# GpSimd waits by semaphore for the vector instruction planned before it at their shared port

## The chip, the cores and the metric

The kernel runs on one core of a Trainium2 chip. The metric is device time in microseconds of that core, the median of three runs. A core has a tensor engine (TensorE, PE in the profile), a vector engine (VectorE, DVE), a scalar engine (ScalarE, ACT), a general engine (GpSimd, POOL) and a queue engine for transfers (SyncE, SP). Each takes its own instructions strictly in order, and they wait for each other by semaphores. The planner in this kernel treats VectorE and GpSimd as sharing a port to on-chip memory.

## The reference

Attention by random features over 8 batches, 8 heads, 576 positions and 64 dimensions with 128 features, and behind it a bilinear feed-forward part over the 4608 tokens of width 512:

```python
def phi(x):                                     # q and k, scaled by 64 ** -0.25
    h = einsum('bhsd,md->bhsm', x, omega) - sum(x * x, -1) / 2
    return exp(h - max(h, -1)) / sqrt(m)
kv  = einsum('bhsm,bhsd->bhmd', phi(k), v)
num = einsum('bhsm,bhmd->bhsd', phi(q), kv)
den = einsum('bhsm,bhm->bhs', phi(q), sum(phi(k), 2)) + 1e-6
x = (num / den) as 4608 x 512
out = ((x @ w1) * (x @ w2)) @ w3 @ w_out        # 512 -> 1024 -> 1024 -> 512
```

## The kernel before

The 4608 tokens are 36 chunks of 128. For precision most matrix operands are split into two 16-bit halves, a high part and the rest, and each product is made of three: high by high, high by low, low by high. So nearly every tensor passes a step that writes the high part (mostly ScalarE) and one that writes the rest (VectorE or GpSimd).

For each chunk the kernel loads q, k and v; splits them (hl, vhl); projects q and k on TensorE into PSUM (pa); takes the maximum (s_nm on VectorE), subtracts it (e on VectorE or within ScalarE's exponential), and splits the result into eq and ek. GpSimd writes most of the low parts of eq and ek by a tensor_tensor of 128x1024 in `in_parts`. The halves of eq are turned by transfers (eqT) and multiplied with kv; VectorE divides (xs), and the result is scaled, split (xhl) and turned by transfers (xT). From chunk 6 on two chunks go together: `pair_turn` lets GpSimd form four sums of xs (128x256 each), after which ScalarE writes the high parts of two xhl tiles and VectorE the rest. The gate multiplies xT with w1 and w2 in a scheme of seven products a pair (weights in w12b, sums of weights in mag); results pass ScalarE and VectorE as asb; GpSimd makes some of their products and the low part of the hidden tile (big). The last product with the joined weights Wb gives the output, which ScalarE scales (o). GpSimd also writes constants into vhl by small memsets.

Nothing runs as written: class `Plan` records every operation with its tiles, then `order` tries several list schedules with estimated costs and returns all operations in the order of their planned starts. `Plan.locks` names those that it takes to need the shared port: everything that GpSimd computes, and VectorE's instructions with wide operands in on-chip memory only (not those that read or write PSUM, no reductions). `forward` never lets two of these overlap in the plan. `fill` adds dummy matmuls in long planned gaps of the first 200 us. `emit` calls `Op.fire` for each operation: the instruction is tied behind its predecessor on its own engine, and `held` lists other operations whose end it waits for by semaphore. Before the change `held` serves a few first loads alone. On the chip nothing else keeps the two engines to the planned turns at the port: each starts when its own data are there.

All instructions are issued from one helper line, L172, so the profile's rows are told apart by tile and shape.

Of the kernel before, what the change touches and what calls it, by code (L numbers as in the profile page):

```python
# [249 lines left out]
class Plan:  # L250
# [77 lines left out]
    def cost(self, op):  # L328
# [20 lines left out]
        if op.lane == "vector":  # L349
# [7 lines left out]
            else:  # L357
                t = 68 + 0.53 * m + 45 * len(thin)
            return t * MARGIN, t * MARGIN + 85
        if op.lane == "scalar":  # L360
            t = (51 if any(a.space == PSUM for a in op.ins) else 93) + 0.834 * m + 92 * len(thin)
            t += 70 if "accum_out" in op.kwargs else 0
            return t * MARGIN, t * MARGIN + 95
        if op.method == "memset":
# [3 lines left out]
        else:  # L368
            t = 100 + 1.0 * m
        return t * MARGIN, t * MARGIN + 50  # L370

# [115 lines left out]
    def order(self):  # L487

        ops = self.ops
        costs = {o: self.cost(o) for o in ops}  # L490
        for o in ops:
            o.locks = self.locks(o)

        def turned(deps):
            after = {o: [] for o in ops}
            for o in ops:
                for d in deps[o]:
                    after[d].append(o)
            return after

        rank = {o: o.index for o in ops}
        best = None
        self.seen = []
        plain = {o: set(o.deps) for o in ops}
        later = turned(plain)
        scale = TURN0
        dice = random.Random(SEED)
        for n in range(ROUNDS + TRIES):
            if n >= ROUNDS:
                rank = {o: r + dice.gauss(0.0, SPREAD) for o, r in best[3].items()}  # L510
            tried = rank
            start, total, slot = self.forward(rank, plain, later, costs, True, scale=scale)
            self.seen.append(total)
            deps = self.chained(start, slot)
            after = turned(deps)
            for m in range(INNER + 1):
                if m:
                    start, total, _ = self.forward(rank, deps, after, costs, scale=1.0)
                    self.seen.append(total)
                if best is None or total < best[0]:  # L520
                    best = total, start, slot, tried
                back = {o: -start[o] - costs[o][0] for o in ops}
                late, _, _ = self.forward(
                    back,
                    {o: set(after[o]) for o in ops},
                    {o: list(deps[o]) for o in ops},
                    costs,
                    backwards=True,
                )
                rank = {o: -late[o] - costs[o][0] for o in ops}  # L530
                scale = 1.0
        _, start, slot, _ = best
        for g, k in slot.items():
            g.slot = k
        start = dict(start)
        self.fill(start, costs)
        return sorted(start, key=lambda o: (start[o], o.index))

    def fill(self, start, costs):


        busy = {}
        for g in self.gens:
            if g.ops and g.tag == "pm":
                a = min(start[o] for o in g.ops)
                b = max(start[o] + costs[o][0] for o in g.ops) + 2 * HOP + 170
                busy.setdefault(g.slot, []).append((a, b))
        line = sorted((o for o in self.ops if o.lane == "tensor"), key=lambda o: start[o])
        end = FIRST
        for o in line:  # L550
            a, b = end, start[o]
            end = b + costs[o][0]
            n = int((b - a - GAP) // 216)
            if n <= 0 or a > UNTIL:
                continue
            idle = [
                (max([y for x, y in t if y <= a + HOP] + [0]), k)
                for k, t in busy.items()
                if not any(x < b and y > a for x, y in t)
            ]  # L560
            if not idle:
                continue
            gen = Gen(self.bank_pool, "pm", [128, 512], F32, 4)
            gen.slot = min(idle)[1]
            out = View(gen, gen.pool.base(gen, gen.slot))
            stuff = Op("tensor", "matmul", (), {})
            stuff.parts = [
                Op("tensor", "matmul", (out, self.ones, self.ones[:, 0:1].broadcast_to([128, 512])),
                   {"start": True, "stop": True})
                for _ in range(n)  # L570
            ]
            stuff.index = o.index
            start[stuff] = a + 1
# [17 lines left out]
SPLIT = True  # L591
HOP = 80
MARGIN = 1.04
ROUNDS = 2
TRIES = 14
SPREAD = 500.0
# [1036 lines left out]
```

## Time and profile before

| what | value |
|---|---|
| device time, median of 3 runs | 767.67 us (766.59 to 767.84) |
| the profiled execution | 767.67 us |
| its span in the trace | 765.9 us |
| PE busy | 742.4 us (97%) |
| DVE busy | 561.1 us (73%) |
| ACT busy | 529.4 us (69%) |
| POOL busy | 317.0 us (41%) |

A busy time counts an instruction from its start to its end, so it holds the time in which an engine stands inside an instruction. Idle time is put down to the instruction or transfer whose end released the engine. The shares are means over very different stages: VectorE is nearly full from 100 to 360 us and has little to do in the last 150, where TensorE works alone. The windows view gives the busy times stage by stage, the waits view who was waited for, and the timeline single instructions; names are the program's tiles, written tile first, then what is read.

### The profile page before, as it was taken

The page shows a single profiled execution, that of the slowest core. Times are in us where ns is not written, and L with a number is a line of the kernel's source. Part 1 is how long each engine was busy: PE and PEld are TensorE (multiplying, and loading weights), DVE is VectorE, ACT ScalarE, POOL GpSimd, SP SyncE. Part 2 cuts the span into 40 slices and gives each one's busy share as a digit, 9 for nine tenths or more (in the row PEclk, how much of TensorE's full clock was granted, in tenths as well). Part 3 has the DMA queues.
Part 4 walks back from the last instruction along what each step waited for, and adds up shares of the span by engine and source line. Part 5 has one row for each costly group of instructions (what it writes and reads, how often), then busy time and mean ns, then how long its engine had stood idle before and what let it go on. Part 6 is the DMA issues. An engine that isn't in the chain of part 4 may idle for free.

```text
span 765.9 us, 24815 instructions
## 1 busy us (share of the span) xinstructions
PE 742.4 (97%) x10639; PEld 579.4 (76%) x10639; DVE 561.1 (73%) x1078; ACT 529.4 (69%) x1069; POOL 317.0 (41%) x306
## 2 busy tenths in 40 slices
PE   8999999999999899988999999999999999999998
PEld 4455678968777879776978877887768887878885
DVE  4568999998999998998898799869773644422220
ACT  6999969878777988877887979966764444322221
POOL 1100102216455475655767645754553434412321
PEclk9999999999999999999999999999999999999999
DMA  9889984426432785545656556661545233312101
GB/s 337 298 311 304 247 183 86 75 67 153 105 58 71 159 170 131 118 98 126 139 144 128 118 115 153 131 122 40 114 78 95 62 87 64 63 43 50 43 15 42
DMA packets 165678, 94.60 MB, mean 124 GB/s; under 512 B 139776, under 2 KB 140160, under 8 KB 165568
## 3 DMA queue, kind: packets, MB, share of 16 engines
q1 hardware_dynamic: 165056, 91.97, 51.2%
q8 instruction: 83, 1.36, 0.8%
q10 hardware_dynamic: 432, 0.79, 0.3%
q14 instruction: 27, 0.22, 0.1%
q0 software_dynamic: 80, 0.26, 0.1%
HBM read 49.35 MB, written 9.44 MB: 77 GB/s over the span
## 4 chain that ended last, share of the span: by engine, by line
PE 63%; DVE 22%; DMA 6%; ACT 6%; issue 3%; SPq 0%; DVEq 0%; ACTq 0%
PE pm L172 53%; PE pa L172 10%; DMA xT<-xhl 4%; DVE s_nm L172 3%; DVE xhl L172 3%; DVE asb L172 2%; DVE big L172 2%; DVE hl L172 2%; ACT e L172 2%; DVE vhl L172 2%; DVE e L172 2%; DVE w12b L172 1%; DVE s_mx L172 1%; DVE xs L172 1%; DMA big<-w3T 1%
## 5 line engine op out<-in xcount | busy, mean ns | idle before, releaser
L172 PE MATMUL pm<-xT,w12b 128*128 128x128 f16 (+1 forms) x3840 | 245.4, 223 | 3.8 <-DMA xT<-xhl 2.4
L172 PEld LDWEIGHTS <-w12b 128*128 128x128 f16 x3840 | 227.6, 98 | 13.7 <-issue 2.8
L172 PE MATMUL pm<-Wb,big 128*128 128x512 f16 (+1 forms) x888 | 192.1, 373 | 0.0
L172 PEld LDWEIGHTS <-big 128*128 128x128 f16 x888 | 85.0, 98 | 92.8 <-issue 0.7
L172 PE MATMUL pm<-xT,mag 128*128 128x128 f16 x2160 | 136.1, 220 | 2.9 <-ACT asb L172 2.8
L172 PEld LDWEIGHTS <-mag 128*128 128x128 f16 x2160 | 124.6, 98 | 6.6 <-issue 3.5
L172 POOL TENSOR_TENSOR big<-asb,big 128x512 f16<-128x512 f32 x72 | 91.7, 1283 | 90.2 <-ACT big L172 71.1
L172 POOL TENSOR_TENSOR eq<-e,eq 128x1024 f16<-128x1024 f32 x31 | 69.5, 2243 | 96.8 <-DVE eq L172 67.7
L172 DVE TENSOR_REDUCE s_nm<-pa 128x8 f32<-128x1024 f32 x72 | 86.7, 1216 | 24.1 <-PE pa L172 23.6
L172 ACT ACTIVATE e<-pa,s_nm,s_es 128x128 f32<-128x128 f32 x240 | 87.9, 465 | 10.6 <-DVE s_nm L172 9.5
L172 POOL TENSOR_TENSOR ek<-e,ek 128x1024 f16<-128x1024 f32 x28 | 63.2, 2256 | 65.0 <-ACT ek L172 49.5
L172 POOL TENSOR_TENSOR asb<-asb,asb 128x512 f32<-128x512 f32 x30 | 40.0, 1332 | 109.4 <-DVE asb L172 100.0
L172 DVE SCALAR_TENSOR_TENSOR asb<-pm,asb 128x512 f32<-128x512 f32 x60 | 41.1, 685 | 50.2 <-PE pm L172 49.7
L172 DVE TENSOR_TENSOR asb<-pm,asb 128x512 f32<-128x512 f32 x72 | 48.8, 681 | 38.9 <-PE pm L172 38.3
L172 ACT CAST big<-asb 128x512 f16<-128x512 f32 x72 | 43.8, 621 | 48.3 <-DVE asb L172 35.0
L172 DVE SCALAR_TENSOR_TENSOR xhl<-xs,s_p2r,xhl 128x768 f16<-128x768 f32 (+2 forms) x36 | 50.3, 1396 | 26.7 <-ACT xhl L172 26.7
L172 PE MATMUL pm<-mag,mag 128*128 128x512 f32 x128 | 58.7, 601 | 0.0
L172 ACT ACTIVATE xhl<-xs,s_p2r 128x768 f16<-128x768 f32 (+2 forms) x36 | 35.8, 993 | 32.3 <-DMA xT<-xhl 25.5
L172 POOL TENSOR_TENSOR xs<-xs 128x256 f32<-128x256 f32 x60 | 48.0, 816 | 21.2 <-DVE xs L172 18.9
L172 ACT ACTIVATE o<-pm,oscs 128x512 f32<-128x512 f32 (+1 forms) x37 | 25.2, 680 | 41.4 <-PE pm L172 39.1
L172 ACT COPY asb<-pm 128x512 f32<-128x512 f32 x60 | 34.9, 592 | 24.0 <-POOL big L172 13.0
L172 PE MATMUL pa<-om,hl 64*128 64x128 f16 x1320 | 45.6, 217 | 4.9 <-DVE xs L172 3.7
(115 smaller groups left out, 1040.2 us busy)
## 6 DMA issues: line engine op xcount, KB each, us to landing
vraw<-v SPq DMA_DIRECT2D x36, 256.0 KB, 3.9
qraw<-qT SPq DMA_DIRECT2D x35, 256.0 KB, 2.8
out<-o SPq DMA_DIRECT2D x34, 256.0 KB, 3.1
big<-w3T SPq DMA_DIRECT2D x8, 1024.0 KB, 7.5
kraw<-kT SPq DMA_DIRECT2D x32, 256.0 KB, 2.9
big<-w SPq DMA_DIRECT2D x8, 1024.0 KB, 7.0
big<-wo SPq DMA_DIRECT2D x3, 1024.0 KB, 5.8
eqT<-eq SPq DMA_TRANSPOSE x72, 3.5
```

The source lines that it names most:

```text
L172: p.real = getattr(lanes[p.lane], p.method)(*args, **{k: real(a) for k, a in p.kwargs.items()})
```

## The change

After the planning a new step, `turns`, walks through all port-using operations in the order of their planned starts. It remembers the last one of VectorE. Each GpSimd operation that follows gets that one into its `held` list, if it doesn't depend on it by its data anyway and if its planned start lies less than `NEAR` = 2500 ns behind the planned end of the vector operation. The tensor order, the tiles, the buffers and every engine's order of instructions stay the same. 179 of GpSimd's operations get such a wait: 56 memsets of vhl, one of mag, 35 low parts of eq and ek, 33 sums of xs and 54 instructions on asb (products and low parts of big). GpSimd's program has 109 semaphore instructions after it, and 72 before; ScalarE's has two fewer.

```diff
--- before.py
+++ after.py
@@ -534,7 +534,17 @@
             g.slot = k
         start = dict(start)
         self.fill(start, costs)
+        self.turns(start, costs)
         return sorted(start, key=lambda o: (start[o], o.index))
+
+    def turns(self, start, costs):
+
+        last = None
+        for o in sorted((o for o in self.ops if o.locks), key=lambda o: (start[o], o.index)):
+            if o.lane == "vector":
+                last = o
+            elif last and last not in o.deps and start[o] - start[last] - costs[last][0] < NEAR:
+                o.held.append(last)
 
     def fill(self, start, costs):
 
@@ -591,6 +601,7 @@
 SPLIT = True
 HOP = 80
 MARGIN = 1.04
+NEAR = 2500.0
 ROUNDS = 2
 TRIES = 14
 SPREAD = 500.0
```

Two places on GpSimd's queue, written as instruction, output<-inputs, size, and in brackets the engines whose semaphores the instruction waits for (DMAHW is a transfer; the numbers only name the counters, and the value waited for is not shown). The first is at 200.7 to 215 us of the trace: eq0 and ek are low parts of features, big0 the low parts of hidden tiles. Before:

```order
L172 TENSOR_TENSOR eq0_101<-e1_305,eq0_101 128x1024 [waits DMAHW2_49,Activation_49]
L172 TENSOR_TENSOR big0_77<-asb2_465,big0_77 128x512 [waits Activation_49]
L172 TENSOR_TENSOR ek4_410<-e0_90,ek4_410 128x1024 [waits Activation_49]
L172 TENSOR_TENSOR big0_77<-asb1_419,big0_77 128x512 [waits Activation_49]
L172 TENSOR_TENSOR eq0_101<-e1_305,eq0_101 128x1024 [waits DMAHW0_49,DVE_49]
L172 TENSOR_TENSOR ek5_671<-e0_90,ek5_671 128x1024 [waits Activation_49]
```

and now:

```order
L172 TENSOR_TENSOR eq0_101<-e1_305,eq0_101 128x1024 [waits DMAHW2_49,DVE_49]
L172 TENSOR_TENSOR big0_77<-asb2_465,big0_77 128x512 [waits Activation_49]
L172 TENSOR_TENSOR ek4_410<-e0_90,ek4_410 128x1024 [waits DVE_49,Activation_49]
L172 TENSOR_TENSOR big0_77<-asb1_419,big0_77 128x512 [waits DVE_49,Activation_49]
L172 TENSOR_TENSOR eq0_101<-e1_305,eq0_101 128x1024 [waits DMAHW0_49,Pool_49]
L172 TENSOR_TENSOR ek5_671<-e0_90,ek5_671 128x1024 [waits DVE_49,Activation_49]
```

The order is the same. The first eq0, the ek parts and the second big0 now wait for VectorE as well. Where a wait vanished from a row, as on the second eq0, a row ahead of it waits for a later vector instruction already.

The second is at 330 to 351 us; xs0 are the four sums of a pair. Before:

```order
L172 TENSOR_TENSOR eq0_101<-e1_305,eq0_101 128x1024 [waits DMAHW4_49,DVE_49,Pool_49]
L172 TENSOR_TENSOR ek3_328<-e0_90,ek3_328 128x1024 [waits Activation_49]
L172 TENSOR_TENSOR big0_77<-asb1_419,big0_77 128x512
L172 TENSOR_TENSOR xs0_105<-xs0_105 128x256 [waits DVE_49]
L172 TENSOR_TENSOR big0_77<-asb2_465,big0_77 128x512 [waits Activation_49,Pool_49]
L172 TENSOR_TENSOR xs0_105<-xs0_105 128x256 [waits Pool_49]
L172 TENSOR_TENSOR xs0_105<-xs0_105 128x256 [waits DVE_49]
L172 TENSOR_TENSOR xs0_105<-xs0_105 128x256 [waits Pool_49]
L172 TENSOR_TENSOR eq0_101<-e1_305,eq0_101 128x1024 [waits DMAHW5_49,DVE_49]
L172 TENSOR_TENSOR asb0_89<-asb0_89,asb1_419 128x512
```

and now:

```order
L172 TENSOR_TENSOR eq0_101<-e1_305,eq0_101 128x1024 [waits DVE_49,DMAHW4_49,Activation_49,Pool_49]
L172 TENSOR_TENSOR ek3_328<-e0_90,ek3_328 128x1024 [waits Activation_49]
L172 TENSOR_TENSOR big0_77<-asb1_419,big0_77 128x512
L172 TENSOR_TENSOR xs0_105<-xs0_105 128x256 [waits DVE_49]
L172 TENSOR_TENSOR big0_77<-asb2_465,big0_77 128x512 [waits Activation_49,Pool_49]
L172 TENSOR_TENSOR xs0_105<-xs0_105 128x256 [waits Pool_49]
L172 TENSOR_TENSOR xs0_105<-xs0_105 128x256 [waits DVE_49] x2
L172 TENSOR_TENSOR eq0_101<-e1_305,eq0_101 128x1024 [waits DMAHW5_49,DVE_49,Activation_49]
L172 TENSOR_TENSOR asb0_89<-asb0_89,asb1_419 128x512
```

Again nothing moved. The first eq0 and the last waited for VectorE before, for their own high part, and wait for a later vector instruction now; the fourth xs0 waited for GpSimd's third sum only, and now for VectorE (equal rows are shown as one, with x2).

## Rows read from the trace of the kernel before

Times in a timeline are us from the span's start.

**Rows 1.** Stage, length, busy us (count) of PE, PEld, DVE, ACT, POOL; clock, DMA, GB/s.
```profile
195.00:255.00 60.00, 53.72 (x827) 43.72 (x825) 59.76 (x105) 43.19 (x87) 32.83 (x31) 0.98 0.39 86
299.00:355.00 56.00, 51.34 (x846) 41.00 (x842) 54.14 (x100) 45.24 (x90) 33.92 (x33) 1.00 0.55 126
355.00:555.00 200.00, 196.59 (x3319) 162.66 (x3313) 168.57 (x329) 157.95 (x315) 119.01 (x112) 0.99 0.55 117
555.00:671.00 116.00, 114.38 (x1752) 92.80 (x1749) 61.15 (x132) 52.16 (x101) 49.31 (x43) 1.00 0.40 74
```

**Rows 2.** Timeline of VectorE, 329 to 355: start us, duration us, instruction, count.
```profile
330.55 5.17 DVE L172 SCALAR_TENSOR_TENSOR vhl<-vraw,s_s,vhl 128x512 f16<-128x512 f32 x2
...
343.47 0.75 DVE L172 SCALAR_TENSOR_TENSOR vhl<-vraw,s_s,vhl 128x512 f16<-128x512 f32 x1
...
345.46 1.01 DVE L172 SCALAR_TENSOR_TENSOR xhl<-xs,s_p2r,xhl 128x768 f16<-128x768 f32 x1
...
349.01 3.15 DVE L172 SCALAR_TENSOR_TENSOR xhl<-xs,s_p2r,xhl 128x1024 f16<-128x1024 f32 x1
352.09 1.75 DVE L172 SCALAR_TENSOR_TENSOR vhl<-vraw,s_s,vhl 64x512 f16<-64x512 f32 x1
353.76 0.67 DVE L172 TENSOR_TENSOR xs<-pa,s_gr 128x512 f32<-128x512 f32 x1
```

**Rows 3.** Timeline of VectorE, 518 to 521.
```profile
518.92 1.28 DVE L172 SCALAR_TENSOR_TENSOR xhl<-xs,s_p2r,xhl 128x1024 f16<-128x1024 f32 x1 [1.21 <-ACT xhl L172]
```

**Rows 4.** Timeline of GpSimd, 329 to 355 (in brackets: idle before).
```profile
330.10 2.52 POOL L172 TENSOR_TENSOR eq<-e,eq 128x1024 f16<-128x1024 f32 x1 [5.37 <-issue]
...
338.63 2.11 POOL L172 TENSOR_TENSOR xs<-xs 128x256 f32<-128x256 f32 x3
348.51 2.57 POOL L172 TENSOR_TENSOR eq<-e,eq 128x1024 f16<-128x1024 f32 x1 [7.77 <-DVE eq L172]
```

**Rows 5.** Timeline of VectorE: first and last blocked instructions, and one at 544.
```profile
195.47 1.22 DVE L172 CAST eq<-e 128x1024 f16<-128x1024 f32 x1
...
250.24 3.14 DVE L172 SCALAR_TENSOR_TENSOR xhl<-xs,s_p2r,xhl 128x1024 f16<-128x1024 f32 x1
...
309.87 0.47 DVE L172 TENSOR_SCALAR s_nm<-s_nm,s_es 128x8 f32<-128x8 f32 x1
...
544.66 2.10 DVE L172 TENSOR_SCALAR s_nm<-s_nm,s_es 128x8 f32<-128x8 f32 x1
```

**Rows 6.** What TensorE waited for in 195 to 255: us, times, longest.
```profile
PE pm L172 <- ACT asb L172: 0.6, 1, 0.6
PE pm L172 <- ACT junk L172: 0.6, 1, 0.6
```

**Rows 7.** What TensorE waited for, 299 to 355.
```profile
PE pm L172 <- ACT asb L172: 0.4, 1, 0.4
```

**Rows 8.** What TensorE waited for, 355 to 555.
```profile
PE pm L172 <- ACT asb L172: 1.5, 2, 1.3
PE pa L172 <- DVE xs L172: 0.8, 2, 0.5
```

**Rows 9.** The same view as rows 1, in two stretches behind idle spells of TensorE.
```profile
253.00:257.00 4.00, 3.72 (x40) 3.72 (x41) 3.90 (x8) 2.44 (x5) 1.16 (x1) 0.57 0.81 182
355.00:359.00 4.00, 4.00 (x51) 3.90 (x45) 3.02 (x4) 2.85 (x6) 1.67 (x2) 0.57 0.25 46
```

**Rows 10.** Timeline of TensorE, 355 to 361.
```profile
355.27 2.58 PE L172 MATMUL pm<-xT,mag 128*128 128x128 f16 x24
...
359.58 1.50 PE L172 MATMUL pm<-xT,mag 128*128 128x128 f16 x24
```

**Rows 11.** Timeline of ScalarE, 329 to 355.
```profile
347.57 1.17 ACT L172 ACTIVATE xhl<-xs,s_p2r 128x1024 f16<-128x1024 f32 x1
```

**Rows 12.** Timeline of GpSimd, 517 to 521.5.
```profile
519.12 0.92 POOL L172 MEMSET vhl<- 64x8 f16 x10
```

**Rows 13.** Groups by line and form, VectorE: count, busy us, mean ns, idle before.
```profile
L172 DVE TENSOR_REDUCE s_nm<-pa 128x8 f32<-128x1024 f32 x72 | 86.7, 1216 | 24.1 <-PE pa L172 23.6
```


## The prediction, made before the changed kernel ran

> **What bounds the kernel now.** Read first the busy times by stage, then what TensorE waits for in each stage, and only then single instructions. By stage [rows 1] TensorE is the busiest engine, but it is not always busy: it stands 60.00 - 53.72 = 6.28 us in 195 to 255, 56.00 - 51.34 = 4.66 us in 299 to 355, 200.00 - 196.59 = 3.41 us in 355 to 555 and 116.00 - 114.38 = 1.62 us in 555 to 671. The reader is to see which engine is full in the two stages that lose most: VectorE, with 59.76 of 60 and 54.14 of 56 us, while GpSimd is at 32.83 and 33.92. So there VectorE sets the end of a step and TensorE waits for it; a microsecond of VectorE given back in those stages shortens the run, until TensorE's own idle time is used up. Elsewhere VectorE has slack and TensorE bounds.
>
> Part of VectorE's full time is not work. Two splits of v in 330.55 take 5.17 us, the same form takes 0.75 alone in 343.47; the split of x in 349.01 takes 3.15 [rows 2], the same form 1.28 in 518.92 [rows 3]. Beside the long ones a GpSimd tensor_tensor began about 0.5 us before: eq in 330.10 and in 348.51 [rows 4]. VectorE's instruction ends when GpSimd's has ended plus its own length: 348.51 + 2.57 = 351.08, plus 1.28 gives 352.36, and it ended in 352.16. So whoever holds the port first makes the other wait. In 195 to 255 there are 12 vector instructions over 75 ns longer than their form's usual time, together 10.7 us; in 299 to 355 there are 8, together 9.2 us (the first and the last of each stage: [rows 2, 5]).
>
> **The change, part by part.** It moves nothing and adds no work to VectorE; it holds 179 GpSimd instructions until the port-using vector instruction planned just before them has ended. A block goes where the GpSimd instruction that made it now waits for the blocked instruction or a later one. Going through the blocked ones with the plan's order, that is so for 10 of the 12 in 195 to 255 (10.0 of 10.7 us), among them those that the first eq0 and the second big0 of the first place shown with the change had blocked, and for 6 of the 8 in 299 to 355 (8.2 of 9.2 us).
>
> One place step by step. The eq in 330.10 now waits for the second of the two v splits. These then take 0.75 each, so VectorE is through in 332.05 and not in 335.72: 3.7 us earlier. GpSimd's eq starts in about 332.1, 2.0 us later, but runs without a block. The eq in 348.51 waits for the half-tile v split of 352.09: VectorE needs 1.28 and about 0.75 us from 349.01 and is through in about 351.0 instead of 353.8, so the xs of 353.76, on which TensorE's longest wait of this stage ends, comes 2.8 us earlier than it did. What is late next is then TensorE itself, with its matmuls before that wait.
>
> By stage, what VectorE gets back (10.0 and 8.2 us) is above what TensorE loses (6.28 and 4.66), so the whole loss could go. I do not count waits that another engine ended and that I can't follow to a blocked vector instruction: in 195 to 255 the two of 0.6 behind ScalarE [rows 6], leaving 6.28 - 1.2 = 5.1; in 299 to 355 the 0.4 behind ScalarE [rows 7], leaving 4.66 - 0.4 = 4.25. In 355 to 555 I count the 0.8 that VectorE's xs ended and 1.3 of the 1.5 behind ScalarE's asb [rows 8], because ScalarE stood there behind the blocked s_nm of 544.66, which took 2.10 us for eight numbers a row [rows 5]: 2.1. In 555 to 671 nothing. Sum 5.1 + 4.25 + 2.1 = 11.45 us.
>
> **The clock.** Right after the two longest idle spells the granted clock falls: 0.57 on the mean in 253 to 257 and in 355 to 359 [rows 9], which is the lower level, 1.2 GHz, for most of each stretch. A group of 24 matmuls takes 2.58 us in 355.27 and 1.50 in 359.58 [rows 10]. At 0.57 four microseconds lose 4 x 0.43 = 1.7, less the little that was idle: 1.6 and 1.7. Both stretches follow spells that the change shortens, so I count both: 3.3 us. Bounds: nothing, if a spell stays long enough to bring the lower level, and 3.3.
>
> **What it costs.** GpSimd starts later. Its added waits have no row before, so from both sides: nothing where the vector instruction has ended anyway, and at most the delay seen by laying the held pairs side by side. The longest is the fourth sum of xs, last of the three in 338.63 [rows 4]. It now waits for the split of x in 345.46, which ends in 346.47 [rows 2]; with 0.70 for the sum it is done in 347.2 and not in 340.74, 6.5 us late. Its reader, ScalarE's xhl, starts in 347.57 [rows 11], so even this one is hidden, by 0.4 us. Behind a held instruction everything on GpSimd's queue stands too, the eq and ek parts and the next sums; GpSimd is idle for 22 of 56 us in this stage, which is the cover [rows 1]. I take nothing for the waits, the value that the longest of them shows, and keep 6 us for the range. TensorE has no wait that GpSimd ended in any of these stages.
>
> Of the 179 waits, 56 hold memsets of vhl. Ten such memsets in 519.12 [rows 12] lie inside the split of x in 518.92, which takes its 1.28 us all the same [rows 3]. The Trainium skill (SBUF — State Buffer, Who interferes with whom) states that a vector instruction with two SBUF inputs contends with a GpSimd instruction that reads SBUF and not with one that only writes it; by that rule these 56 waits buy nothing and only hold GpSimd's queue, and the trace agrees at this place. The sum is the same by rule and by row: no gain was booked for them, and their delay falls under the waits above.
>
> **The sum.** The profiled execution took 767.67 us, which is the median of the three runs too (its span is 765.9, 1.8 lie around it). 767.67 - 11.45 - 3.3 = 752.9 us.
>
> **Rivals.**
> - Half of it. VectorE is freed, but the next thing in line, ScalarE's activations or the transposes of x and eq, ends the step almost as late. For it: ScalarE has 45.24 of 56 us, and part of TensorE's waits in 195 to 255 end on it [rows 1, 6]. Against it: VectorE is given back 1.6 and 1.8 times what TensorE stands (10.0 to 6.28, 8.2 to 4.66). Half of 11.45 and one of the two clock stretches: 767.67 - 5.7 - 1.7 = 760.3 us.
> - The block only moves. GpSimd must read for its 33.9 us within those 56 somewhere, and after the wait it may meet the next port-using vector instruction instead. For it: GpSimd's instructions are up to 2.6 us long and VectorE leaves no gap. Against it: much of VectorE's work does not use the port, such as the reductions from PSUM, at 1216 ns on the mean with 86.7 us in all [rows 13], and the plan lays GpSimd's instructions beside these; holding them brings them back there. It would give 767.7 us, no change.
> - Slower: the sums of xs. They feed ScalarE's xhl, the transpose and TensorE's matmuls, and there is one set of four for each of 15 pairs of chunks. Where the vector instruction waited for is itself late, or ScalarE ready earlier than in 347.57, the 6.5 us of the fourth sum comes through to TensorE save for its 0.4 of cover: 6.1 us a pair. Three such pairs cost 18.3 and outweigh 14.75 of gain: 771.2 us. It decides from the third pair on. For it: cover of 0.4 us is thin. Against it: with VectorE earlier the instruction waited for is earlier too.
>
> **How the numbers follow.** Forecast 0.62, half 0.22, the block moves 0.08, slower 0.08. About 0.2%, 1.5 us, is what a measurement of this kernel can tell from no change. So faster 0.62 + 0.22 = 0.84, same 0.08, slower 0.08. Low end: all of TensorE's idle time in the four stages (15.97) and both clock stretches, 767.67 - 19.3 = 748.4. High end: past half, with the 6 us kept for the waits, 760.3 + 6 = 766.3, up to the edge of no change. That leaves out the last two cases, 0.16, and little below.
>
> **What would show it.** Right: in the changed profile the v splits near 330 take 0.75 each and the x split near 349 takes 1.28; VectorE's busy time falls by some 30 us, GpSimd's idle time ended by VectorE grows; TensorE's idle time in 195 to 355 falls below 4 us; the granted clock has no fall near 253 and 355. Wrong: VectorE's blocked instructions are as many as before, only others (the block moves); ScalarE's xhl waits on GpSimd's xs by several us a pair (slower); or VectorE's time falls and TensorE's waits stay, ended by ScalarE or transposes (half).

## The result, and the profile after

The changed kernel takes 753.59 us (752.89 to 754.26, median of 4), the kernel before 767.15 beside it: ratio 0.9823, 95% interval 0.9806 to 0.984. Forecast were 752.9 us, in a range of 748.4 to 766.3. The profiled execution took 754.26 us with a span of 752.5, so 13.4 us less span than before.

The page's busy times of the changed kernel, engine by engine:

```profile
PE 738.1 (98%) x10639; PEld 576.2 (77%) x10639; DVE 534.7 (71%) x1078; ACT 528.7 (70%) x1069; POOL 296.1 (39%) x306
```

TensorE's idle time went from 765.9 - 742.4 = 23.5 to 752.5 - 738.1 = 14.4 us: 9.1 of the 13.4. The other 4.3 are TensorE's busy time, with as many matmuls; the two falls of the clock [rows 9] are not in this execution. VectorE is busy for 534.7 us and not 561.1, GpSimd for 296.1 and not 317.0, with the same instructions: both stood inside their instructions before.

By stage, in the columns of [rows 1] (the windows are the same times; TensorE's work of before now comes earlier, by 0.2 us at 195, 6 at 253, 10 at 355 and 15 at 555):

```profile
195.00:255.00 60.00, 58.09 (x959) 48.62 (x958) 57.54 (x112) 49.47 (x100) 30.50 (x33) 1.00 0.51 102
255.00:299.00 44.00, 43.06 (x799) 36.28 (x797) 37.77 (x71) 37.61 (x77) 23.09 (x27) 1.00 0.70 147
299.00:355.00 56.00, 54.38 (x806) 41.82 (x802) 48.37 (x106) 48.01 (x99) 30.74 (x24) 1.00 0.68 133
355.00:555.00 200.00, 199.35 (x3389) 163.72 (x3386) 164.38 (x346) 156.42 (x309) 114.78 (x116) 1.00 0.59 118
555.00:671.00 116.00, 113.18 (x1739) 93.52 (x1737) 51.49 (x104) 48.90 (x96) 46.36 (x40) 1.00 0.34 67
```

TensorE stands 1.91, 0.94, 1.62, 0.65 and 2.82 us in them, where it stood 6.28, 0, 4.66, 3.41 and 1.62. VectorE is no longer full in 299 to 355: 48.37 us against 54.14. The granted clock is 1.00 in all five. What TensorE still waits for in 195 to 255, then in 299 to 355, then in 555 to 671 (us, times, longest):

```profile
PE pm L172 <- DMA xT<-xhl: 1.6, 1, 1.6
PE pa L172 <- DMA eqT<-eq: 0.3, 1, 0.3
```

```profile
PE pm L172 <- ACT asb L172: 1.6, 1, 1.6
```

```profile
PE pm L172 <- DVE asb L172: 1.5, 1, 1.5
PE pa L172 <- ACT e L172: 0.6, 2, 0.4
PE pm L172 <- ACT asb L172: 0.5, 1, 0.5
```

In the first two stages none of it ends on VectorE any more. In the last stage the wait that ends on VectorE's asb has grown from 0.7 us to 1.5, and 0.6 behind ScalarE's e is new.

The place that the prediction went through, on VectorE and then on GpSimd, answers to [rows 2] and [rows 4]:

```profile
323.55 1.41 DVE L172 SCALAR_TENSOR_TENSOR vhl<-vraw,s_s,vhl 128x512 f16<-128x512 f32 x2
...
337.02 1.02 DVE L172 SCALAR_TENSOR_TENSOR xhl<-xs,s_p2r,xhl 128x768 f16<-128x768 f32 x1 [1.32 <-ACT xhl L172]
...
341.07 1.28 DVE L172 SCALAR_TENSOR_TENSOR xhl<-xs,s_p2r,xhl 128x1024 f16<-128x1024 f32 x1
342.26 0.74 DVE L172 SCALAR_TENSOR_TENSOR vhl<-vraw,s_s,vhl 64x512 f16<-64x512 f32 x1
342.93 0.68 DVE L172 TENSOR_TENSOR xs<-pa,s_gr 128x512 f32<-128x512 f32 x1
```

```profile
325.19 2.14 POOL L172 TENSOR_TENSOR eq<-e,eq 128x1024 f16<-128x1024 f32 x1 [6.48 <-DVE s_gd L172]
327.28 2.14 POOL L172 TENSOR_TENSOR ek<-e,ek 128x1024 f16<-128x1024 f32 x1
...
338.12 0.73 POOL L172 TENSOR_TENSOR xs<-xs 128x256 f32<-128x256 f32 x1 [4.42 <-DVE s_gd L172]
343.14 2.13 POOL L172 TENSOR_TENSOR eq<-e,eq 128x1024 f16<-128x1024 f32 x1 [4.29 <-ACT junk L172]
```

The two v splits take 1.41 us and not 5.17, and GpSimd's eq starts in 325.19, when the second has ended. The x split takes 1.28 and not 3.15, the half-tile v split 0.74 and not 1.75; the eq behind them starts in 343.14 and takes 2.13 without a block. The fourth sum of xs waits for the split in 337.02 and is done in 338.85. Its reader on ScalarE:

```profile
339.62 1.18 ACT L172 ACTIVATE xhl<-xs,s_p2r 128x1024 f16<-128x1024 f32 x1
```

It starts in 339.62, 0.8 us later: hidden, as forecast. What is not gone: 34 vector instructions are still over 75 ns longer than usual, together 16.2 us, where it was 54 and 44.7 us (the sum over the single instructions of the timeline, against the usual length of their form). The longest, on VectorE and on GpSimd:

```profile
273.59 2.83 DVE L172 SCALAR_TENSOR_TENSOR xhl<-xs,s_p2r,xhl 128x1024 f16<-128x1024 f32 x1
```

```profile
273.22 2.13 POOL L172 TENSOR_TENSOR ek<-e,ek 128x1024 f16<-128x1024 f32 x1 [3.09 <-DVE xhl L172]
```

GpSimd's ek waits for one vector instruction here and meets the next one of the plan. But this pair stood in each other's way before as well; VectorE, then GpSimd, in the trace of before:

```profile
280.55 2.58 DVE L172 SCALAR_TENSOR_TENSOR xhl<-xs,s_p2r,xhl 128x1024 f16<-128x1024 f32 x1
```

```profile
279.91 2.13 POOL L172 TENSOR_TENSOR ek<-e,ek 128x1024 f16<-128x1024 f32 x1 [3.42 <-ACT ek L172]
```

VectorE's order is the same in both kernels, so its instructions can be laid side by side one by one. About half of the 16 us, on 15 instructions, is on such as were blocked before; the other half, some 8 us on 18, is on such as were not. So the rival in which the block moves is real for 8 of 45 us, 2 of them in the two main stages.

The reduction from PSUM, which the plan lays beside GpSimd's work, is as long as in [rows 13], 1219 ns to 1216:

```profile
L172 DVE TENSOR_REDUCE s_nm<-pa 128x8 f32<-128x1024 f32 x72 | 86.9, 1219 | 25.7 <-PE pa L172 25.1
```

### The profile page after: what moved, and what is told of

Read it like the earlier page. It is cut to its first block, busy times and chain, and to the rows that moved or that the text cites. A ratio compares the mean times of both kernels' runs of the same rounds, so it can differ in the third digit from the quotient of the medians.

```text
span 752.5 us, 24850 instructions
## 1 busy us (share of the span) xinstructions
PE 738.1 (98%) x10639; PEld 576.2 (77%) x10639; DVE 534.7 (71%) x1078; ACT 528.7 (70%) x1069; POOL 296.1 (39%) x306
## 4 chain that ended last, share of the span: by engine, by line
PE 73%; DVE 8%; ACT 7%; DMA 7%; issue 3%; POOL 1%; SPq 0%; DVEq 0%; ACTq 0%; POOLq 0%
PE pm L172 62%; PE pa L172 11%; DMA xT<-xhl 4%; ACT e L172 2%; DVE s_nm L172 1%; DMA big<-w3T 1%; DMA big<-wo 1%; DMA vraw<-v 1%; DVE hl L172 1%; ACT ek L172 1%; DVE asb L172 1%; DVE xhl L172 1%; ACT vhl L172 1%; ACT xhl L172 1%; ACT asb L172 1%
## 5 line engine op out<-in xcount | busy, mean ns | idle before, releaser
L172 PE MATMUL pm<-xT,mag 128*128 128x128 f16 x2160 | 134.5, 219 | 2.3 <-ACT asb L172 2.1
L172 POOL TENSOR_TENSOR big<-asb,big 128x512 f16<-128x512 f32 x72 | 82.7, 1158 | 99.8 <-ACT big L172 39.7
L172 DVE TENSOR_REDUCE s_nm<-pa 128x8 f32<-128x1024 f32 x72 | 86.9, 1219 | 25.7 <-PE pa L172 25.1
L172 POOL TENSOR_TENSOR eq<-e,eq 128x1024 f16<-128x1024 f32 x31 | 66.2, 2134 | 79.1 <-DVE eq L172 33.0
L172 POOL TENSOR_TENSOR ek<-e,ek 128x1024 f16<-128x1024 f32 x28 | 59.8, 2135 | 63.1 <-DVE ek L172 13.6
L172 POOL TENSOR_TENSOR asb<-asb,asb 128x512 f32<-128x512 f32 x30 | 38.1, 1271 | 111.2 <-DVE asb L172 94.6
L172 DVE SCALAR_TENSOR_TENSOR xhl<-xs,s_p2r,xhl 128x768 f16<-128x768 f32 (+2 forms) x36 | 42.3, 1175 | 31.4 <-ACT xhl L172 31.0
L172 POOL TENSOR_TENSOR xs<-xs 128x256 f32<-128x256 f32 x60 | 44.9, 761 | 36.0 <-DVE xs L172 9.4
```

The costliest lines, as they stand in the source:

```text
L172: p.real = getattr(lanes[p.lane], p.method)(*args, **{k: real(a) for k, a in p.kwargs.items()})
```

## Experiments

Eleven kernels ran. "Blocked" is the time by which port-using vector instructions are longer than usual, by the same measure as above; "two stages" is the part planned for 190 to 246 and 289 to 346 us, which runs at about 195 to 255 and 299 to 355. Times are medians beside runs of the kernel before.

| run | this, us | before, us | ratio (95%) | blocked, us | in the two stages |
|---|---|---|---|---|---|
| before (profile) | | 767.15 | | 44.7 | 19.9 |
| changed | 753.59 | 767.15 | 0.9823 (0.9806 to 0.984) | 16.2 | 3.5 |
| e1 memsets only | 767.39 | 767.01 | 1.001 (0.9993 to 1.0026) | 43.8 | 20.0 |
| e2 no memsets | 754.06 | 767.01 | 0.9845 (0.9816 to 0.9875) | 14.4 | 3.5 |
| e3 two stages | 755.39 | 767.01 | 0.9856 (0.9834 to 0.9877) | 26.2 | 3.4 |
| e4 elsewhere | 764.61 | 767.01 | 0.9969 (0.9953 to 0.9985) | 32.5 | 20.0 |
| e5 two back | 758.26 | 766.72 | 0.9882 (0.9859 to 0.9905) | 34.9 | 12.0 |
| e6 writes only | 749.48 | 766.72 | 0.9777 (0.976 to 0.9793) | 0.8 | 0.0 |
| e7 no limit | 755.28 | 766.72 | 0.9849 (0.9828 to 0.987) | 14.4 | 3.4 |
| e8 features only | 757.35 | 766.72 | 0.9874 (0.9856 to 0.9892) | 33.2 | 9.6 |
| e9 writes and waits | 750.65 | 768.00 | 0.9757 (0.9734 to 0.978) | 0.2 | 0.0 |
| e10 four back | 768.84 | 768.00 | 1.0008 (0.9992 to 1.0024) | 47.3 | 21.1 |
| e11 halves | 754.87 | 768.00 | 0.9822 (0.9796 to 0.9849) | 18.1 | 4.9 |

Three theories stood against each other: the waits gain because VectorE is not blocked where it sets the pace (theory); blocked time given back counts wherever it is; and holding GpSimd back gains by itself (pacing).

**e1 and e2: which instructions must wait.** The condition in `turns` is narrowed to memsets, and to all but memsets.

```diff
-            elif last and last not in o.deps and ...
+            elif o.method == "memset" and last and last not in o.deps and ...      # e1; e2 has !=
```

> Only the 57 memsets keep their wait. Theory (the waits gain because GpSimd's reads no longer stand in VectorE's way): a memset reads nothing and blocked no vector instruction in the trace of before, so none of the 38.3 us of blocked time is covered: 767 us, within 1.5 of before, and about 54 vector instructions still blocked. Rival (any holding back of GpSimd gains, by pacing it): 57 of 179 waits give a third of 13.6 us: 762.6.

> The 122 waits that are not on memsets. Theory: all 38.3 us of covered blocks stay covered: 753.6, within 1.5. If the memset waits cost something on GpSimd's queue, below 752. Rival (pacing): two thirds of 13.6 us: 758.1.

e1 is no change, e2 is the changed kernel within what can be told. In e1 the long splits on VectorE are all there, the pair of v splits and the x split of [rows 2]:

```profile
330.24 5.17 DVE L172 SCALAR_TENSOR_TENSOR vhl<-vraw,s_s,vhl 128x512 f16<-128x512 f32 x2
...
348.71 3.15 DVE L172 SCALAR_TENSOR_TENSOR xhl<-xs,s_p2r,xhl 128x1024 f16<-128x1024 f32 x1
```

So 57 of the 179 waits do nothing, and pacing by count is refuted at this point. This agrees with the rule of the Trainium skill that the prediction weighed (SBUF — State Buffer, Who interferes with whom: a GpSimd instruction that only writes does not contend with a vector instruction with two SBUF inputs). e1 alone shows only that these waits are not needed; that writes block nothing, longer ones too, is shown by e6 below.

**e3 and e4: where the waits are needed.** By planned start:

```diff
-            elif last and last not in o.deps and ...
+            elif (190e3 <= start[o] < 246e3 or 289e3 <= start[o] < 346e3) and last and ...   # e3; e4 has not (...)
```

> Only the 41 waits planned for 190 to 246 and 289 to 346 us, which run at about 195 to 255 and 299 to 355. Theory (a block costs only where VectorE sets the pace): 5.1 + 4.25 us of TensorE's idle time and 3.3 us of the lower clock, 12.65 in all: 754.5, though they cover just 19.1 of the 38.3 us. Rival (gain in proportion to the blocked time given back, wherever it is): half of 13.6: 760.4. Rival (pacing, by count of waits): 41 of 179: 764.

> The other 138 waits, which cover the other 19.1 us of blocks. Theory: only the 2.1 us of 355 to 555 and no clock: 765.0. Rival (in proportion to blocked time): 760.4. Rival (pacing, by count): 756.7.

41 waits bring 11.6 us, the other 138 bring 2.4, though these give back 12.2 of 44.7 us of blocked time. The windows show why, in the columns of [rows 1]; first e3, then e4:

```profile
195.00:255.00 60.00, 58.00 (x958) 48.59 (x957) 57.21 (x112) 49.53 (x99) 30.52 (x33) 1.00 0.53 102
299.00:355.00 56.00, 54.73 (x827) 42.07 (x824) 47.98 (x107) 49.26 (x100) 30.99 (x25) 1.00 0.68 133
355.00:555.00 200.00, 196.34 (x3340) 161.93 (x3335) 170.52 (x337) 155.31 (x307) 121.73 (x115) 1.00 0.59 117
```

```profile
195.00:255.00 60.00, 53.52 (x843) 43.71 (x841) 59.76 (x105) 43.11 (x86) 32.64 (x31) 1.00 0.39 86
299.00:355.00 56.00, 51.36 (x847) 40.99 (x842) 54.19 (x101) 45.49 (x90) 33.80 (x33) 1.00 0.59 126
355.00:555.00 200.00, 199.25 (x3346) 163.00 (x3340) 163.43 (x333) 158.85 (x316) 111.33 (x113) 1.00 0.59 118
```

In e3 TensorE stands 2.00 and 1.27 us in the two stages and 3.66 in 355 to 555, in e4 6.48 and 4.64, but 0.75 in 355 to 555. Each set of waits takes TensorE's idle time away where it is. The rival that counts blocked time wherever it is gave 760.4 for both and is refuted.

That e4 comes out near its forecast of 765.0 is in part luck. Of the 2.7 us that it gains in 355 to 555, 1.73 come back as idle time in 255 to 299, where before had none, and 0.64 in 555 to 671. TensorE's idle time in the whole profile is as before (23.6 and 23.5 us); the span is 4.1 us shorter because TensorE's busy time is 738.2 and not 742.4 us: this execution has neither of the two falls of the clock.

The traces also answer the rival of pacing in another way. For each of GpSimd's 306 instructions one can count how many of VectorE's have started by then. Against before, GpSimd is later by this count in 143 instructions in the changed kernel, in 38 in e1, 36 in e3 and 110 in e4. The gains are 13.6, none, 11.6 and 2.4 us: they do not go with how much of GpSimd's work is held back.

**e5 and e10: the same instructions wait, for the wrong one.** Each waits for the port-using vector instruction two turns, or four turns, further back.

```diff
+                past.append(o)
-                o.held.append(last)
+                if len(past) > BACK:
+                    o.held.append(past[-1 - BACK])          # BACK = 2 in e5, 4 in e10
```

> The same 179 GpSimd instructions wait, but for the port-using vector instruction two turns further back. Laid on the trace of before, such waits come after only 8 of the 54 blocked instructions, 5.6 of 44.7 us, 3.3 of it in 195 to 255 and none in 299 to 355. Theory: 2 to 4 us faster than before, 763 to 765. Rival (the wait itself, its pacing of GpSimd's queue): most of the gain stays, 754 to 758.

> The 179 instructions wait for the port-using vector instruction four turns further back. Laid on the trace of before such waits come after none of the 54 blocked instructions. The run with two turns back gave more (758.3) than its static cover, because 9.8 us of blocked time went there. Theory: blocked time and the time go together again; with almost no wait that binds, 40 us and more stay blocked and the time is 764 to 767. Rival (that GpSimd waits for VectorE at all is what gains): 754 to 760.

e5 missed the theory's number: 8.5 us faster and not 2 to 4. The expectation had laid the waits on the old trace and counted only blocks that a wait rules out. VectorE and GpSimd in e5 show what else they do:

```profile
326.29 3.29 DVE L172 SCALAR_TENSOR_TENSOR vhl<-vraw,s_s,vhl 128x512 f16<-128x512 f32 x2
...
343.34 1.27 DVE L172 SCALAR_TENSOR_TENSOR xhl<-xs,s_p2r,xhl 128x1024 f16<-128x1024 f32 x1
344.53 2.61 DVE L172 SCALAR_TENSOR_TENSOR vhl<-vraw,s_s,vhl 64x512 f16<-64x512 f32 x1
```

```profile
326.50 2.52 POOL L172 TENSOR_TENSOR eq<-e,eq 128x1024 f16<-128x1024 f32 x1 [5.41 <-issue]
...
343.55 3.04 POOL L172 TENSOR_TENSOR eq<-e,eq 128x1024 f16<-128x1024 f32 x1 [3.55 <-ACT junk L172]
```

The eq of 326.50 starts 0.2 us behind the first v split, that of 343.55 0.2 us behind the x split: it has lost the race that it had won before. So the x split takes 1.27, the pair of v splits 3.29 (the second one still blocked), and the half-tile v split behind is blocked, 2.61. A wait on an older instruction need not rule a block out to change who comes first. Blocked time in the two stages falls from 19.9 to 12.0 us and TensorE's idle time to 2.15 and 1.71, nearly as far as in the changed kernel, where blocked time fell to 3.5. So there, too, a block counts only as far as TensorE stands for it:

```profile
195.00:255.00 60.00, 57.85 (x908) 48.22 (x907) 58.60 (x110) 47.96 (x96) 36.63 (x33) 0.97 0.49 104
299.00:355.00 56.00, 54.29 (x859) 42.98 (x854) 53.97 (x108) 47.59 (x93) 34.65 (x24) 1.00 0.61 125
```

In e10 GpSimd wins the race as before, and the blocks are as before; VectorE, then GpSimd:

```profile
333.67 5.17 DVE L172 SCALAR_TENSOR_TENSOR vhl<-vraw,s_s,vhl 128x512 f16<-128x512 f32 x2
...
352.61 3.16 DVE L172 SCALAR_TENSOR_TENSOR xhl<-xs,s_p2r,xhl 128x1024 f16<-128x1024 f32 x1
```

```profile
333.23 2.53 POOL L172 TENSOR_TENSOR eq<-e,eq 128x1024 f16<-128x1024 f32 x1 [5.59 <-issue]
...
352.11 2.57 POOL L172 TENSOR_TENSOR eq<-e,eq 128x1024 f16<-128x1024 f32 x1 [4.16 <-DVE eq L172]
```

With as many waits as in the changed kernel, no gain: the waits themselves neither gain nor cost. They hardly hold GpSimd back, though (16 of its 306 instructions are later, counted as above), so against pacing e1, e3 and e4 say more.

**e6 and e9: GpSimd reads nothing.** In the kernel before (e6) and in the changed kernel (e9) each GpSimd tensor_tensor is a memset of its output; the low parts, sums and products that it made are left out.

```diff
-            p.real = getattr(lanes[p.lane], p.method)(*args, ...)
+            if p.lane == "gpsimd" and p.method == "tensor_tensor":
+                p.real = lanes[p.lane].memset(args[0], 0.0)      # and waits for the producers of its inputs
+            else:
+                p.real = getattr(lanes[p.lane], p.method)(*args, ...)
```

> The kernel before, without the change; each GpSimd tensor_tensor is a memset of the same output at the same place that waits for the same inputs, so GpSimd reads nothing (the low parts, sums and products that it made are left out; its instructions also get shorter). Theory: no vector instruction is blocked any more, VectorE's busy time falls by about 44 us to 517, TensorE's idle time in 195 to 355 as with the waits or less: 750 to 754. If being blocked were not the port but GpSimd's running at all: VectorE's long instructions stay and the time is 760 or more.

> The changed kernel, and each GpSimd tensor_tensor a memset of the same output that waits for the same inputs and for the same vector instruction as in the changed kernel (the low parts, sums and products that GpSimd made are left out). So the waits are there and nothing is left that could block VectorE. Theory (the waits gain by the port alone): no gain from them, 749.5 within 1.5, as with the memsets and no waits. Rival (pacing of GpSimd): the waits gain here too, 8 to 13 us more: 737 to 742.

e6 needs no waits and is faster than the changed kernel, by a little more than was expected. Its page, and its two stages:

```profile
PE 736.9 (99%) x10639; PEld 575.5 (77%) x10639; DVE 520.8 (70%) x1078; ACT 527.9 (71%) x1069; POOL 131.9 (18%) x306
```

```profile
195.00:255.00 60.00, 58.46 (x967) 49.10 (x966) 55.27 (x111) 49.64 (x100) 13.25 (x31) 1.00 0.51 103
299.00:355.00 56.00, 56.00 (x851) 43.39 (x849) 48.12 (x108) 50.87 (x104) 14.37 (x26) 1.00 0.70 140
```

VectorE falls by 40.3 us to 520.8, and TensorE stands 1.54 us in the first stage and not at all in the second. e9 has the waits as well and gains nothing by them:

```profile
195.00:255.00 60.00, 58.49 (x952) 48.61 (x952) 55.30 (x112) 49.36 (x100) 13.68 (x33) 1.00 0.53 104
299.00:355.00 56.00, 56.00 (x851) 43.38 (x849) 48.12 (x109) 49.48 (x102) 14.16 (x25) 1.00 0.70 138
```

With the port out of the way the same waits are worth nothing. As a control on pacing this is weak, because in e6 TensorE has only 3.9 us of idle time left from 195 to 671 us, so a gain of 8 to 13 us could not have come. e6 also bounds the change: about 749.5 us is what no blocking gives, of which the waits reach 753.6. Part of the difference of 4 us may be GpSimd's shorter instructions in e6; that was not taken apart.

**e7, e8 and e11: how many, which, how long.** e7 lifts the limit (`NEAR = 1e9`), e8 holds only the 128x1024 low parts, e11 issues these in two halves with the wait on the first.

> The limit of 2.5 us is lifted: 282 waits in place of 179. Laid on the trace of before the 103 more cover no further block. Theory: no change from the changed kernel, 753.6 within 1.5. [...]

> Only the 35 long instructions (low parts of eq and ek, 2.1 us each) wait. They cover 11 blocked instructions but 18.4 us: 5.1 in 195 to 255, 6.6 in 299 to 355, 6.7 in 355 to 555. Theory: 5.1 and 4.25 us of TensorE's idle time could still go and the two falls of the clock with them, so 754 to 757. Rival (in proportion to blocked time): 18.4 of 38.3 of 13.6 us: 760.6. Rival (by count): 35 of 179: 764.5.

> The changed kernel, and the 59 GpSimd tensor_tensors of 128x1024 are issued as two of 128x512, the wait on the first. Theory: a vector instruction that still meets one stands for 1.1 us at most and not 2.1, so the 16.2 us still blocked fall to 10 to 13; TensorE still stood 1.9 us in 195 to 255 and 1.6 in 299 to 355, so at best 1 to 2 us: 751.5 to 753.6. Rival (blocks that are left cost nothing, the new instructions do): 754 to 757.

e7: 103 more waits change nothing that can be told (755.28 against 753.59, just outside of what was expected; but the ratios to the runs of before beside them, 0.985 and 0.982, have intervals that overlap). e8: 35 of the 179 waits give 9.4 us, just short of what the theory gave and far from both rivals; blocked time in the two stages falls to 9.6. e11 missed its theory: no gain over the changed kernel (ratio 0.9822 to 0.9823), and blocked time did not fall to 10 to 13 us but is 18.1, where the changed kernel has 16.2; whether the halves take the port twice stays open. None of the kernels that compute the whole reference beats the changed one.

## Why the prediction was right, step by step

- VectorE full in two stages, partly standing at the port: shown. Its busy time fell by 26.4 us, where some 30 were forecast. e3 against e4 places 11.6 of the gain there, and e6 takes the standing away without any wait.
- A block goes when GpSimd's instruction waits for the blocked one or a later one: shown in the rows of 323 to 343 us, each within 0.1 us of the lengths forecast. The step missed that late GpSimd instructions meet the next vector instruction: of the 10.0 and 8.2 us counted as given back, the two stages got 16.4 of 18.2.
- TensorE's idle time, 11.45 us: this term was too large. Between the profiles it fell by 9.1, but 1.0 of that is at the very start and brought nothing, because the same 172 matmuls are busy 1.05 us longer there (before, then changed):

```profile
0.00:35.00 35.00, 31.48 (x172) 15.75 (x173) 17.26 (x39) 27.71 (x69) 5.33 (x16) 1.00 0.88 321
```
```profile
0.00:35.00 35.00, 32.53 (x172) 16.45 (x173) 17.28 (x39) 28.00 (x70) 5.26 (x16) 1.00 0.88 322
```

That leaves 8.0. The two main stages and 355 to 555 gave 4.37, 3.04 and 2.76 us, 10.2 where 11.45 were booked; 0.94 in 255 to 299 and 1.2 in 555 to 671 came back, behind ScalarE's e and VectorE's asb. The stages were taken one by one, but what is gained in one can make TensorE wait in the next. Part may also be the price of the waits: e3, which holds nothing in these two stretches, stands only 0.05 and 1.05 us there (the changed kernel 0.94 and 2.82). No run takes the two apart.
- The clock, 3.3 us: the size was right, the reason not. The profile of before has both falls and the changed one neither. Laid side by side, matmul by matmul, the work of the two stretches of [rows 9] is busy 3.92 and 3.98 us before and 2.41 and 2.34 now, 3.2 less. But a fall does not follow from an idle spell as the prediction had it. The spell that came before the first fall was not shortened by the change, 1.65 us before and 1.63 now, and the lower level stayed away all the same; the group of 24 takes 1.51 us and not 2.74:

```profile
253.28 2.74 PE L172 MATMUL pm<-xT,w12b 128*128 128x128 f16 x24 [1.65 <-DMA xT<-xhl]
```
```profile
247.53 1.51 PE L172 MATMUL pm<-xT,w12b 128*128 128x128 f16 x24 [1.63 <-DMA xT<-xhl]
```

And e4 has the spell that came before the second fall, as long as it was, and no fall behind it. TensorE's row of before, then the two of e4, then e4's clock:

```profile
354.49 0.85 PE L172 MATMUL pa<-om,hl 64*128 64x128 f16 x24 [2.08 <-DVE xs L172]
```
```profile
354.61 0.85 PE L172 MATMUL pa<-om,hl 64*128 64x128 f16 x24 [2.08 <-DVE xs L172]
355.38 1.51 PE L172 MATMUL pm<-xT,mag 128*128 128x128 f16 x24
```

```profile
355.00:359.00 4.00, 4.00 (x82) 3.90 (x76) 3.78 (x6) 2.86 (x6) 1.66 (x2) 1.00 0.19 38
```

The group of 24 takes 1.51 us, the granted clock is 1.00. So that this term came true is luck, for the first fall above all. Of 19 executions of the kernel before, beside e1 to e4, the four with a mean granted clock of 1.000 took 764.5 to 765.1 us, the others 766.0 to 769.9; by these the kernel before loses 2.3 us at the median (767.0 against 764.7), and not a set 3.3. It is not the whole of the spread: of the 13 executions beside e9 to e11 the two at 1.000 took 766.4 and 767.2 us, the others 766.5 to 770.1. Beside the same runs, e2's two executions at 1.000 took 753.55 and 753.69 us, so with full clock on both sides the waits are worth about 11 us.
- The waits for nothing: the fourth sum of xs is 0.8 us ahead of its reader, and e7 with 103 more waits costs nothing that can be told; whether the waits cost something in 255 to 299 and 555 to 671 stays open, as said. The times of e1 and e2 show that the 56 memsets neither gain nor cost.
- The signs that the prediction named: GpSimd's idle time that VectorE ended grew, from 238 to 372 us, and the granted clock fell near neither 253 nor 355. One sign failed: TensorE's idle time in 195 to 355 was to fall below 4 us and went from 10.94 to 4.47, over the mark by what came back in 255 to 299.
- The rivals: half of it fell. Slower fell, as VectorE's own lead brought the awaited instruction earlier too (337.02 and not 345.46); ScalarE's xhl waits for GpSimd's xs 5.5 us in the whole run, where it was 3.8. The block moves holds for 8 of 45 us of blocked time, most of it outside the two stages that count.

So the mechanism, its places and its sign were right. That the sum came so near, 14.75 us forecast and 13.4 between the profiles, is partly luck: the idle time gave 3.4 us less than was booked, and 2.1 us came that were not booked at all. These are busy time of TensorE outside the two falls, 1.2 of them in 195 to 253. They go where idle time goes (in e4, whose idle time there stays, the same matmuls of 195 to 253 are as long as before); why, no run shows.

## What to carry to other kernels

Where two engines share a port, look for instructions whose length varies with one form: the row with the long one, laid beside the other engine's timeline, shows who came first. Let the engine that has idle time wait for the one that is full, and only where that one sets the pace: here 41 of 179 waits brought 11.6 of the 13.6 us. Test such a gain with the same number of waits on the wrong instruction and with the port use taken out; a count of blocks on the old trace alone misjudges what a wait does to the order in which two engines reach the port.

## What the runs showed of the hardware that was not expected

- A start 0.2 us behind the other engine's was enough to lose the port: in e5 GpSimd's eq 0.2 us behind VectorE's x split took 3.04 us where it takes 2.13 alone, and the split its usual 1.27.
- A blocked instruction ends a little before the end of GpSimd's plus its own length, and by a steady amount: the x split in 349.01 by 0.20 us (352.16 and not 352.36). In the eleven traces in which GpSimd reads it is 0.19 to 0.21 us for 232 of 246 blocked splits (scalar_tensor_tensor) and 0.13 to 0.15 us for all 230 blocked casts, tensor_tensor and tensor_scalar instructions.
- GpSimd's busy time fell by 20.9 us without a change of its work: it stood at the port too (the eq of 330.10 took 2.52 us, that of 325.19 2.14), and its rows give no other sign of it than their length.
- The lower clock came or stayed away behind the same work and the same idle spell: 2.08 us in before and in e4, 0.57 granted behind it in [rows 9], 1.00 in e4; and between executions of one program, of which four in 19 kept a mean of 1.000.
